# Clustered attention and a rational MoE layer on one core: new instruction sequences on every engine, and ones-matmuls over 128 rows

## The chip, the core and the metric

The kernel runs on one core of a Trainium2 chip. Five engines run their own instruction queues in order: PE (TensorE, matmuls), DVE (VectorE), ACT (ScalarE), POOL (GpSimd) and SP (SyncE, which here only issues DMAs). The metric is the device time of one execution in microseconds. Three runs of the kernel before gave 928.95, 930.76 and 934.13, median 930.76. A fourth execution was profiled; its own time is 927.86, its span in the trace 926.1.

## The reference

```python
# q, k, v: 4 batches x 8 heads x 768 tokens x 64; centroids: 8 heads x 16 x 64
q_assign = argmax(normalized(q) . normalized(centroids)); k_assign likewise
scores = (q @ k.T) / 8, set to -1e9 where q_assign != k_assign
attn   = softmax(scores);  x = attn @ v      # -> 3072 tokens x 512
h = x @ w_in                                  # 512 x 2048
P = a0 + a1*h + a2*h^2 + a3*h^3
Q = 1 + |b0|*|h| + |b1|*h^2
out = (P / (Q + 1e-6)) @ w_out                # 2048 x 512
```

## The kernel before, in words

**Tiles.** Heads are taken in four pairs per batch, tokens in six tiles of 128 per head. q and k are split into two fp16 parts with 64 further rows: the cluster of a token is written there as a one-hot row of large numbers, so that one matmul gives score and mask. `prep` does this for a pair: it loads q and k (`rk`, `rq`), squares them on ACT with a sum (`sumk`, `sumq`, tile `tk` as scratch), and finds the largest sum over the partitions. For that `over_partitions` (L960 to L968) transposes the sums on PE (`kt`, `qt`, L964), takes the maximum on DVE (`km`, `qm`, L966; tag `m1`), and spreads that one number over 128 partitions by a matmul with a row of ones (`kb`, `qb`, L968). The scale for v does the same (L785, L787, L790). Powers of two come from it (`ksc`, `qsc`), ACT and DVE write the split (`tk`, `tq`), a DMA transpose issued by SP ("turn", L1059) puts the features on the partitions (`sk`, `sq`), 48 small matmuls against the centroids give `ptl` (L1085), DVE and POOL make the one-hot `oh` of it (L1099 to L1109, L1116), and two more turns bring the second parts.

**Attention.** Batch 0 computes scores with keys on the partitions (`attend_keys`): scores for the maxima (L1301, DVE `top` L1310), the maxima written back as rows of q and turned once more, second scores `z` (L1362), exp on ACT, then `px` in fp32 (L1381, L1387). The other batches (`attend`) take 128 queries a time: scores `s` (L1181), maximum on DVE (L1197), exp on ACT with sum `su`, a split into two fp16 parts `ah` by ACT and DVE (L1234), a turn each (L1241, tile `at`), and `px` (L1254). A PSUM buffer of scores is free again when the DVE half of `ah` has read it, and two of them serve this.

**MoE.** x goes through w_in (`ph`, L1511), the rational function on ACT, DVE and POOL in pieces of 512 (`u`, `t`, `s`), and w_out (`po`, L1622). Weights are loaded and split into parts by ACT, DVE (L669 to L681) and POOL (L750, L757) in the first 200 us, beside attention of batch 0. Constants of the rational function, `g` and `gk`, are worked out one number at a time on DVE and POOL (L833, L871).

**Order.** Nothing of this runs in the order of the source. Every step is recorded with `op`: engine, an assumed duration, function, buffers read and written. `Plan.order` then brings the records into one program. A table `ORDER` holds for every engine the full list of step numbers, and each engine's steps come out in the order of its list (801 steps on PE, 1400 on DVE, 989 on ACT, 609 on POOL, 356 on SP). The assumed durations (`DMA`, `QUEUE`, `SWITCH`, the number in each `op`) then only decide which buffer of a ring a tile gets. On the chip each engine takes its list from the front and waits there for data and buffers.

Of the kernel before, what the change touches and what calls it, by code (L numbers as in the profile page):

```python
# [27 lines left out]
K = {'ghd': 0.0, 'rvp': 0, 'look': 62.89, 'mulp': 0.4, 'sub': 0, 'xn': 14, 'NR': 8, 'sgp': 1, 'scp': 1, 'vsc': 0.75, 'sup0': 0, 'stk': 2, 'lop': 0, 'mgp': 0, 'rvn': 2, 'tq2': 2, 'at': 3, 'es': 4, 'vn': 3, 'ah': 5, 'rel': 0, 'twin': 1}  # L28
# [171 lines left out]
class Plan:  # L200
# [1542 lines left out]
```

## Time and profile before

| | |
|---|---|
| runs, median (lowest to highest) | 930.76 us (928.95 to 934.13) |
| profiled execution: time, span | 927.86 us, 926.1 us |
| PE busy | 859.2 us, 93% of the span |
| DVE, ACT, POOL busy | 809.5, 763.8, 604.0 us |
| mean granted TensorE clock | 0.991 of full |
| chain that ended last | PE 28%, DVE 3%, every other engine 1% or less |

Read it by stretches: in the first 75 us PE is busy 37 us, because loads, prep and the first turns come one after the other. From 75 on it is over 90% busy, save for 50 us after 200, where batch 0's attention has ended and batch 1's begins. From 250 to 900 PE stands still for 7 us in all.

### The profile page before, as it was taken

How to read it: one execution, taken by the hardware profiler on the slowest of the kernel's cores; microseconds unless marked ns; L12 is line 12 of the kernel's file. 1: busy time of each engine (PE TensorE's matmuls, PEld its weight loads, DVE VectorE, ACT ScalarE, POOL GpSimd, SP SyncE). 2: the span in 40 equal slices, each digit the busy share in tenths (PEclk: the TensorE clock that was granted, in tenths of full speed). 3: DMA queues.
4: the chain of work that ended last, by engine and by line, in shares of the span. 5: the costliest groups of instructions: out<-in, count | busy, mean ns of one | idle time of the engine just before them, and what ended most of it. 6: DMA issues, size and time to landing. Idle time of an engine off the chain costs nothing. (4 is left out here: it accounts for less than half of the span.)

```text
span 926.1 us, 20282 instructions
## 1 busy us (share of the span) xinstructions
PE 859.2 (93%) x7705; PEld 586.4 (63%) x7705; DVE 809.5 (87%) x1618; ACT 763.8 (82%) x1182; POOL 604.0 (65%) x627
## 2 busy tenths in 40 slices
PE   1559998997999999999999999999999999999997
PEld 1346675765676666667667676666666667766664
DVE  5789899658999999999999999999999998777776
ACT  5656675878998999998999999999998898766674
POOL 1347627398888776888888788868877766322221
PEclk9979999999999999999999999999999999999999
DMA  9996774666677797886869698898758667500000
GB/s 280 295 259 186 171 172 125 184 135 148 124 131 166 138 202 145 165 168 156 157 110 201 123 168 167 173 145 169 161 107 163 123 140 107 83 24 24 1 24 23
DMA packets 357345, 132.95 MB, mean 144 GB/s; under 512 B 335104, under 2 KB 351488, under 8 KB 357248
## 3 DMA queue, kind: packets, MB, share of 16 engines
q1 hardware_dynamic: 357248, 131.67, 67.5%
q8 instruction: 60, 0.98, 0.4%
q14 instruction: 37, 0.30, 0.1%
HBM read 41.98 MB, written 6.29 MB: 52 GB/s over the span
## 5 line engine op out<-in xcount | busy, mean ns | idle before, releaser
L1622 PE MATMUL po<-wout,u 128*128 128x512 f16 x1152 | 266.1, 379 | 1.4 <-ACT ob L526 0.8
L1511 PE MATMUL ph<-x,win 128*128 128x256 f16 x2304 | 266.1, 273 | 1.2 <-DVE x L1270 0.9
L1511 PEld LDWEIGHTS <-win 128*128 128x128 f16 x2304 | 225.1, 98 | 39.7 <-issue 3.2
L1551 POOL TENSOR_TENSOR s<-s,u 128x512 f32<-128x512 f32 x96 | 131.0, 1382 | 117.9 <-ACT s L526 85.7
L1622 PEld LDWEIGHTS <-u 128*128 128x128 f16 x1152 | 111.0, 98 | 122.2 <-issue 3.4
L1234 DVE SCALAR_TENSOR_TENSOR ah<-s,su,ah 128x768 f16<-128x768 f32 x144 | 143.3, 1012 | 8.9 <-ACT ah L526 7.5
L1197 DVE TENSOR_SCALAR_CACHE_REDUCE s<-s,cc 128x768 f32<-128x768 f32 x144 | 144.6, 1018 | 7.4 <-PE s L1181 6.8
L526 ACT ACTIVATE ah<-s,su 128x768 f16<-128x768 f32 x144 | 127.1, 904 | 15.3 <-ACT s L526 7.2
L526 ACT ACTIVATE s<-s,nm 128x768 f32<-128x768 f32 x144 | 126.5, 879 | 12.8 <-DVE s L1197 9.6
L1574 POOL TENSOR_TENSOR s<-s,u 128x512 f32<-128x512 f32 x72 | 103.5, 1448 | 28.7 <-ACT u L526 28.5
L1181 PE MATMUL s<-sk,sq 128*128 128x384 f16 x576 | 113.6, 328 | 8.5 <-DVE ah L1234 3.9
L1611 POOL TENSOR_TENSOR u<-s,u 128x512 f16<-128x512 f32 x72 | 86.5, 1213 | 30.6 <-ACT u L526 16.9
L1181 PEld LDWEIGHTS <-sq 128*128 128x128 f16 x576 | 52.7, 98 | 52.3 <-DVE ah L1234 13.0
L1254 PE MATMUL px<-at,vhi 128*64 128x256 f16 x864 | 74.8, 275 | 1.2 <-DVE df L1100 0.7
L526 ACT ACTIVATE u<-ph 128x512 f32<-128x512 f32 x96 | 57.5, 601 | 19.9 <-PE ph L1511 19.4
L1532 DVE TENSOR_TENSOR t<-ph,t 128x512 f32<-128x512 f32 x96 | 65.4, 682 | 9.0 <-ACT t L526 8.7
L1254 PE MATMUL px<-at,vlo 128*64 128x256 f16 x432 | 61.3, 273 | 0.0
L1604 DVE SCALAR_TENSOR_TENSOR s<-s,t 128x1024 f32<-128x1024 f32 (+1 forms) x49 | 58.7, 1197 | 1.7 <-POOL s L1574 0.7
L1254 PEld LDWEIGHTS <-vhi 128*64 128x64 f16 x864 | 47.9, 110 | 15.7 <-issue 8.2
L526 ACT ACTIVATE u<-t 128x1024 f16<-128x1024 f32 (+1 forms) x49 | 51.2, 1045 | 6.1 <-DVE t L1594 3.0
L526 ACT ACTIVATE t<-ph,gk 128x512 f32<-128x512 f32 x72 | 56.1, 784 | 0.0
L1537 DVE SCALAR_TENSOR_TENSOR t<-t,gk,ph 128x512 f32<-128x512 f32 x72 | 53.0, 740 | 0.9
(213 smaller groups left out, 1520.7 us busy)
## 6 DMA issues: line engine op xcount, KB each, us to landing
rwi<-in_moe_w_in_dram SPq DMA_DIRECT2D x16, 512.0 KB, 5.4
rwo<-in_moe_w_out_dram SPq DMA_DIRECT2D x16, 512.0 KB, 5.4
rk<-in_k_dram SPq DMA_DIRECT2D x32, 192.0 KB, 3.3
rq<-in_q_dram SPq DMA_DIRECT2D x32, 192.0 KB, 3.0
rvm<-in_v_dram SPq DMA_DIRECT2D x16, 384.0 KB, 5.6
rv<-in_v_dram SPq DMA_DIRECT2D x16, 384.0 KB, 4.0
out_dram<-ob SPq DMA_DIRECT2D x11, 512.0 KB, 3.2
at<-ah SPq DMA_TRANSPOSE x144, 3.9
```

What stands on the lines that cost most here:

```text
L526: lambda: nc.scalar.activation(out=out(), in_=in_(), func=func, **{a: (x() if callable(x) else x) for a, x in kw.items()}),
L1181: nc.tensor.matmul(sc.ap[:, i, :SH], lhsT=st["q" + x].ap[:, j, t, :], rhs=st["k" + x].ap[:, j, ks, :].rearrange("p t c -> p (t c)"), start ...
L1197: lambda nm=nm, view=view: ts(out=view(), in0=view(), scalar1=cc.ap, scalar2=None, op0=ALU.mult, op1=ALU.min, accum_out=nm.ap),
L1234: lambda part=part, view=view, su=su: stt(out=part(1), in0=view(), scalar=su.ap, in1=part(0), op0=ALU.mult, op1=ALU.subtract),
L1254: nc.tensor.matmul(px.ap[j * D : (j + 1) * D, :], lhsT=vv.ap[:, j, kt, :], rhs=at[j].ap[:, p_, kt].rearrange("p t c -> p (t c)"), start=(i ...
L1511: nc.tensor.matmul(ph[i].ap[:, fi * TW : (fi + 1) * TW], lhsT=win[f // 4][:, wpart, c, f % 4 * P : (f % 4 + 1) * P], rhs=xs[c].ap[:, xpart ...
L1532: lambda i=i, th=th, ph=ph: tt(out=th[i].ap, in0=ph[i].ap, in1=th[i].ap, op=ALU.mult),
L1551: lambda i=i, sh=sh, uh=uh: nc.gpsimd.tensor_tensor(out=sh[i].ap, in0=sh[i].ap, in1=uh[i].ap, op=ALU.mult),
L1574: lambda i=i, sh=sh, uh=uh: nc.gpsimd.tensor_tensor(out=sh[i].ap, in0=sh[i].ap, in1=uh[i].ap, op=ALU.mult),
L1604: lambda tw=tw, sw=sw: stt(out=sw(), in0=sw(), scalar=2.0, in1=tw(), op0=ALU.subtract, op1=ALU.mult),
L1611: lambda i=i, sh=sh, gl=gl, g16=g16, e=(nc.vector if gld else nc.gpsimd): e.tensor_tensor(out=gl[i].ap, in0=sh[i].ap, in1=g16()[:, 0, i * ...
L1622: nc.tensor.matmul(po[ti].ap, lhsT=g16()[:, part, c0 : c0 + P], rhs=wout[f // 4][:, wpart, f % 4], start=(k == 0 and f == f_first), stop=( ...
```

## The change

Three things. **1.** `ORDER` is replaced by another table of the same steps: ACT has 592 of 989 steps at another place, DVE 1018 of 1400, PE 379 of 801 (none by more than 10 places), POOL 499 of 609, SP 256 of 356. The last 4 steps of PE and ACT, 12 of DVE, 8 of POOL and 9 of SP are as before. **2.** The 24 ones-matmuls that spread a maximum (20 at L968, 4 at L790) take all 128 rows of `ones`; their right side is a column of 128 numbers, zero but for the first, which DVE writes. Four such columns are set to zero once at the start. **3.** The rest of the diff is not used by this table: a PE way of turning (`by_pe`), a share of DVE (`xl`), a step `avs` that keeps its old value 3, other assumed DMA durations, and an fp16 identity that POOL copies once.

```diff
-K = {... 'twin': 1}
+K = {... 'twin': 1, 'pet': '_', 'avs': 3}
 ORDER = {
     "ACT": """
-369 370 13 383 386 7 15 39 8 17 19 34 1222 29 24 491 492 44 1224 ...
+370 369 13 1222 383 39 386 15 34 17 19 29 7 8 44 491 1224 24 25 ...
-    DMA = {"turn": (1440.0, 4100.0, 1700.0), "w": (430.0, 3900.0, 1350.0), ...
-    QUEUE = 950.0
+    DMA = {"turn": (1500.0, 4100.0, 1750.0), "w": (500.0, 4000.0, 1400.0), ...
+    QUEUE = 1300.0
+    columns = [cp.tile([P, 1], F32, name=f"column{i}") for i in range(4)]
+    def column(name):
+        return Buf(lambda i: (name, columns[i])[1], "m1", len(columns), False)
+    ident16 = cp.tile([P, P], F16, name="ident16")
+    nc.gpsimd.tensor_copy(out=ident16, in_=ident)
+    for x in columns:
+        nc.vector.memset(x, 0.0)
 @@ over_partitions (the scale of v likewise) @@
-            m1 = buf([1, 1], F32, "m1", f"{nm}m{n}", 4)
-            dve(195, lambda: nc.vector.tensor_reduce(out=m1.ap, in_=pt.ap[0:1, :], axis=AX.X, op=ALU.max), [pt], [m1], u)
+            m1 = column(f"{nm}m{n}")
+            dve(195, lambda: nc.vector.tensor_reduce(out=m1.ap[0:1], in_=pt.ap[0:1, :], axis=AX.X, op=ALU.max), [pt], [m1], u)
             pb = misc([P, 1], F32, f"{nm}b{n}")
-            op("PE", 310, lambda: nc.tensor.matmul(pb.ap, lhsT=ones[0:1, :], rhs=m1.ap, start=True, stop=True), [m1], [pb], u, mode=2)
+            op("PE", 310, lambda: nc.tensor.matmul(pb.ap, lhsT=ones, rhs=m1.ap, start=True, stop=True), [m1], [pb], u)
```

Three places show what the table moves. The first is POOL around 196 to 204 us, where it works on weights (`wwo`, `wout`), on x of batch 0 (`x0_...`) and on the constants `g11` and `g10c1`, whose results DVE waits for. Before:

```order
L1440 TENSOR_TENSOR x0_2_2_2454<-rs0_2_2_2354,x0_2_2_2454 128x256
L833 TENSOR_SCALAR g10c0_1086<-g10c0_1086 128x1
L905 TENSOR_TENSOR gk0c0_885<-gk0c0_885,aab_97 128x4
L1116 TENSOR_SCALAR tq21_0_2276<-oh1_0_2610 128x12x64
L833 TENSOR_SCALAR g10c1_2270<-g10c1_2270 128x2
L833 TENSOR_SCALAR g10c1_2270<-g10c1_2270,aab_97 128x1
L833 TENSOR_SCALAR g10c1_2270<-g10c1_2270 128x1
L757 TENSOR_TENSOR wout3_110<-wwo3_0_2095,wout3_110 128x512
L833 TENSOR_SCALAR g11_2318<-g11_2318 128x1
L1154 TENSOR_TENSOR vlo1_0_2659<-rv1_0_799,vhi1_0_2608 128x768
L1440 TENSOR_TENSOR x0_3_0_2701<-rs0_3_0_2560,x0_3_0_2701 128x256
L833 TENSOR_SCALAR g11_2318<-g11_2318,aab_97 128x1
```

After:

```order
L759 TENSOR_SCALAR wwo3_1_2180<-wwo3_1_2180,wos_124 128x512
L842 TENSOR_SCALAR g11_2406<-g11_2406 128x2
L1185 TENSOR_TENSOR vlo1_0_2626<-rv1_0_710,vhi1_0_2612 128x768
L842 TENSOR_SCALAR g11_2406<-g11_2406,aab_107 128x1
L842 TENSOR_SCALAR g11_2406<-g11_2406 128x1
L842 TENSOR_SCALAR g11_2406<-g11_2406,aab_107 128x1
L766 TENSOR_TENSOR wout3_120<-wwo3_0_2085,wout3_120 128x512
L1473 TENSOR_TENSOR x0_2_2_2697<-rs0_2_2_2361,x0_2_2_2697 128x256
L766 TENSOR_TENSOR wout3_120<-wwo3_1_2180,wout3_120 128x512
```

The last `g11` row that reads `aab` stood behind two `x0` rows and a `wout` row; now it is ahead of them.

The second is ACT around 211 to 218 us, the start of batch 1's attention: `s1_...` is the exp of a score tile, `ah1_...` the ACT half of the split behind it, `u0` and `t0` the MoE of batch 0, `tq11_2` and `vhi1_2` prep of batch 1. Before:

```order
L526 ACTIVATE x0_3_2_2840<-rs0_3_2_2727 128x256
L526 ACTIVATE s1_0_0_1_2744,su1_0_0_1_2844<-s1_0_0_1_2744,nm1_0_0_1_2768 128x2x384
L526 ACTIVATE ah1_0_0_0_2866<-s1_0_0_0_2731,su1_0_0_0_2765 128x768
L526 ACTIVATE tq11_2_2741<-rq1_2_2538,qsc1_2_2786 128x12x64
L526 ACTIVATE u0_0_0_2894<-ph0_0_0_0_2770 128x512
L526 ACTIVATE vhi1_2_2904<-rv1_2_2729,ev1_747 128x768
L526 ACTIVATE t0_0_0_2920<-ph0_0_0_0_2770,gk0c0_885 128x512
L526 ACTIVATE ah1_0_0_1_2929<-s1_0_0_1_2744,su1_0_0_1_2844 128x768
L526 ACTIVATE u0_0_0_2894<-ph0_0_0_1_2874 128x512
L526 ACTIVATE s1_0_1_0_2897,su1_0_1_0_2937<-s1_0_1_0_2897,nm1_0_1_0_2925 128x2x384
```

After:

```order
L535 ACTIVATE ah1_0_0_0_2839<-s1_0_0_0_2728,su1_0_0_0_2757 128x768
L535 ACTIVATE x0_3_2_2842<-rs0_3_2_2724 128x256
L535 ACTIVATE s1_0_0_1_2738,su1_0_0_1_2844<-s1_0_0_1_2738,nm1_0_0_1_2764 128x2x384
L535 ACTIVATE tq11_2_2735<-rq1_2_2544,qsc1_2_2762 128x12x64
L535 ACTIVATE vhi1_2_2890<-rv1_2_2726,ev1_653 128x768
L535 ACTIVATE ah1_0_0_1_2897<-s1_0_0_1_2738,su1_0_0_1_2844 128x768
L535 ACTIVATE u0_0_0_2907<-ph0_0_0_0_2825 128x512
L535 ACTIVATE t0_0_0_2924<-ph0_0_0_0_2825,gk0c0_898 128x512
L535 ACTIVATE s1_0_1_0_2899,su1_0_1_0_2929<-s1_0_1_0_2899,nm1_0_1_0_2922 128x2x384
L535 ACTIVATE u0_0_0_2907<-ph0_0_0_1_2877 128x512
```

Each `ah1` row now comes ahead of the `x0`, `u0` and `t0` rows that it followed.

The third is SP around 94 to 109 us, the second turns of batch 0's third pair (`sk20_2`, `sq20_2`) among loads. Before:

```order
L1059 DMA_TRANSPOSE sq20_1_676<-tq20_1_430 128x12x128
L1059 DMA_TRANSPOSE sq20_2_1206<-tq20_2_762 128x12x128
L1059 DMA_TRANSPOSE sk20_2_1276<-tk20_2_844 128x12x128
L1059 DMA_TRANSPOSE sk10_3_1286<-tk10_3_924 128x12x128
L540 DMA rk1_0_1294<-in_k_dram 128x384 x2
L540 DMA rv0_1_1311<-in_v_dram 128x2x384
L540 DMA rwi2_1_1314<-in_moe_w_in_dram 128x1024
L540 DMA rwi2_2_1326<-in_moe_w_in_dram 128x1024
L540 DMA rwi2_3_1351<-in_moe_w_in_dram 128x1024
```

After:

```order
L1089 DMA_TRANSPOSE sq20_1_700<-tq20_1_433 128x12x128
L549 DMA rwi2_3_1168<-in_moe_w_in_dram 128x1024
L1089 DMA_TRANSPOSE sk20_2_1203<-tk20_2_706 128x12x128
L1089 DMA_TRANSPOSE sq20_2_1220<-tq20_2_757 128x12x128
L549 DMA rk1_0_1275<-in_k_dram 128x384
L1089 DMA_TRANSPOSE sk10_3_1279<-tk10_3_931 128x12x128
L549 DMA rk1_0_1275<-in_k_dram 128x384
L549 DMA rwi2_2_1298<-in_moe_w_in_dram 128x1024
L549 DMA rwi2_1_1312<-in_moe_w_in_dram 128x1024
L549 DMA rv0_1_1321<-in_v_dram 128x2x384
```

The load `rwi2_3` stood seven places behind those two turns and stands in front of both now, and k's turn goes before q's.

## Rows read from the trace of the kernel before

**Rows 1.** Busy us by stretch: length, PE, PEld, DVE, ACT, POOL, PEclk, DMA share, GB/s
```profile
0.00:36.00 36.00, 9.45 (x85) 6.86 (x85) 22.14 (x76) 21.53 (x45) 8.60 (x25) 1.00 0.99 298
36.00:75.00 39.00, 27.45 (x191) 17.46 (x193) 33.46 (x74) 21.85 (x41) 16.93 (x21) 0.82 1.04 274
75.00:200.00 125.00, 116.80 (x1469) 84.14 (x1468) 101.53 (x217) 86.93 (x148) 72.69 (x109) 1.00 0.59 149
200.00:250.00 50.00, 40.98 (x393) 29.53 (x393) 43.53 (x103) 42.55 (x70) 42.90 (x54) 0.97 0.74 150
250.00:900.00 650.00, 643.04 (x5453) 436.55 (x5451) 591.88 (x1131) 579.12 (x865) 459.83 (x419) 1.00 0.68 131
```

**Rows 2.** PE timeline, 205:236; start us, us, engine line op, tiles, count [idle before <-releaser]
```profile
206.39 0.27 PE L964 MATMUL kt<-ident,sumk 128*1 128x128 f32 x1 [1.89 <-ACT tk L526]
...
219.15 1.26 PE L1181 MATMUL s<-sk,sq 128*128 128x384 f16 x4 [2.07 <-DVE su L1217]
220.20 4.04 PE L1511 MATMUL ph<-x,win 128*128 128x256 f16 x24
```

**Rows 3.** PE timeline around a one-row ones-matmul inside the MoE stream
```profile
259.92 1.24 PE L1622 MATMUL po<-wout,u 128*128 128x512 f16 x5
261.10 0.38 PE L968 MATMUL kb<-km,ones 1*128 1x1 f32 x2
261.40 1.04 PE L1622 MATMUL po<-wout,u 128*128 128x512 f16 x4
```

**Rows 4.** PE timeline around a 128-row ones-matmul that exists already
```profile
184.65 0.82 PE L1362 MATMUL z<-sq,sk 128*128 128x256 f16 x6
185.30 0.28 PE L708 MATMUL won<-woa,ones 128*128 128x1 f32 x2
185.44 0.81 PE L1362 MATMUL z<-sq,sk 128*128 128x256 f16 x6
```

**Rows 5.** All instructions of the line with 20 of the 24 ones-matmuls, two passes each
```profile
L968 PE MATMUL kb<-km,ones x32: 245/266/368, 9.6 to 666.6; 1*128 1x1 f32 x32
```

**Rows 6.** DVE timeline, one pass over a weight chunk at the start
```profile
17.49 0.69 DVE L674 SCALAR_TENSOR_TENSOR wwi<-rwi,wwi 128x512 int32<-128x512 int32 x1
```

**Rows 7.** PE timeline: second scores of the first pair, scores of the third pair
```profile
65.68 3.81 PE L1362 MATMUL z<-sq,sk 128*128 128x256 f16 x18
...
105.54 2.77 PE L1301 MATMUL s<-sk,sq 128*128 128x384 f16 x16
```

**Rows 8.** POOL timeline, 194:207
```profile
199.64 1.16 POOL L757 TENSOR_TENSOR wout<-wwo,wout 128x512 f16<-128x512 f32 x1
...
202.69 0.67 POOL L1440 TENSOR_TENSOR x<-rs,x 128x256 f16<-128x256 f32 x1
203.35 0.34 POOL L833 TENSOR_SCALAR g<-g,aab 128x1 f32<-128x1 f32 x1
```

**Rows 9.** DVE timeline, 203:220
```profile
203.73 0.21 DVE L871 TENSOR_SCALAR g<-g 128x1 f32<-128x1 f32 x1 [2.00 <-POOL g L833]
...
204.18 1.19 DVE L1052 COPY tk<-tk 128x768 f16<-128x768 f16 x1
...
217.02 0.69 DVE L1532 TENSOR_TENSOR t<-ph,t 128x512 f32<-128x512 f32 x1
...
218.08 1.01 DVE L1234 SCALAR_TENSOR_TENSOR ah<-s,su,ah 128x768 f16<-128x768 f32 x1
```

**Rows 10.** ACT timeline, 205:217
```profile
205.40 0.84 ACT L526 ACTIVATE tk<-rk 128x768 bf16<-128x768 f32 x1 [3.23 <-DVE tk L1052]
```

**Rows 11.** DMA issues in 199.9:201.5; the last number is the us to landing
```profile
sk<-tk SPq DMA_TRANSPOSE x1, 5.0
```

**Rows 12.** SP timeline, 92:112
```profile
99.93 4.77 SPq L1059 DMA_TRANSPOSE sk<-tk  x2
...
106.33 2.95 SPq L540 DMA_DIRECT2D rwi<-in_moe_w_in_dram  x3
```

**Rows 13.** DVE timeline, last pass over the weight chunk whose buffer that load takes
```profile
95.47 1.37 DVE L681 SCALAR_TENSOR_TENSOR wwo<-rwo,wwo 128x512 int32<-128x512 int32 x2
```

More of the change, by code (lines that the diff above doesn't have):

```diff
@@ L25 @@
 M_BIG, M_MID, M_LOW = 2.0 ** 15, 2.0 ** 7, 2.0 ** -4
-K = {'ghd': 0.0, 'rvp': 0, 'look': 62.89, 'mulp': 0.4, 'sub': 0, 'xn': 14, 'NR': 8, 'sgp': 1, 'scp': 1, 'vsc': 0.75, 'sup0': 0, 'stk': 2, 'lop': 0, 'mgp': 0, 'rvn': 2, 'tq2': 2, 'at': 3, 'es': 4, 'vn': 3, 'ah': 5, 'rel': 0, 'twin': 1}
+K = {'ghd': 0.0, 'rvp': 0, 'look': 62.89, 'mulp': 0.4, 'sub': 0, 'xn': 14, 'NR': 8, 'sgp': 1, 'scp': 1, 'vsc': 0.75, 'sup0': 0, 'stk': 2, 'lop': 0, 'mgp': 0, 'rvn': 2, 'tq2': 2, 'at': 3, 'es': 4, 'vn': 3, 'ah': 5, 'rel': 0, 'twin': 1, 'pet': '_', 'avs': 3}
 ORDER = {
     "ACT": """
[32 rows of a table removed]
[32 rows of a table added]
 """,
     "DVE": """
[45 rows of a table removed]
[45 rows of a table added]
 """,
     "PE": """
[26 rows of a table removed]
[26 rows of a table added]
 """,
     "POOL": """
[20 rows of a table removed]
[20 rows of a table added]
 """,
     "SP": """
[11 rows of a table removed]
[11 rows of a table added]
 3803 3811 3196 3925 4035 4153 4154
@@ L206 @@
     MORE = {("ACT", "POOL"): 95.0, ("DVE", "POOL"): 60.0, ("POOL", "ACT"): -30.0, ("ACT", "ACT"): 120.0, ("PE", "DVE"): 65.0, ("DVE", "ACT"): 50.0}
-    DMA = {"turn": (1440.0, 4100.0, 1700.0), "w": (430.0, 3900.0, 1350.0), "v": (450.0, 3900.0, 1100.0),
-           "qk": (430.0, 3000.0, 500.0), "few": (350.0, 2500.0, 200.0), "o2": (340.0, 3800.0, 1310.0), "o1": (340.0, 2300.0, 700.0)}
-    QUEUE = 950.0
+    DMA = {"turn": (1500.0, 4100.0, 1750.0), "w": (500.0, 4000.0, 1400.0), "v": (500.0, 4000.0, 1150.0),
+           "qk": (500.0, 3100.0, 520.0), "few": (350.0, 2500.0, 200.0), "o2": (340.0, 3800.0, 1310.0), "o1": (340.0, 2300.0, 700.0)}
+    QUEUE = 1300.0
     SWITCH = 105.0
@@ L455, in share @@
         return math.floor((i + 1) * f + 1e-6) > math.floor(i * f + 1e-6)
-    KEYMAJOR = {(0, int(hp)) for hp in kn("km", "0123")}
+    KEYMAJOR = {(0, int(hp)) for hp in kn("km", "0123") if hp != "_"}
     plan.look = kn("look", 40.0)
@@ L785, in v_scale @@
         op("PE", 110, lambda: nc.tensor.transpose(out=pt.ap[0:1, :], in_=vm1.ap, identity=ident), [vm1], [pt], vt)
-        m1 = buf([1, 1], F32, "m1", f"vmm{b}", 4)
-        dve(195, lambda: nc.vector.tensor_reduce(out=m1.ap, in_=pt.ap[0:1, :], axis=AX.X, op=ALU.max), [pt], [m1], vt)
+        m1 = column(f"vmm{b}")
+        dve(195, lambda: nc.vector.tensor_reduce(out=m1.ap[0:1], in_=pt.ap[0:1, :], axis=AX.X, op=ALU.max), [pt], [m1], vt)
         pb = misc([P, 1], F32, f"vb{b}")
         op(
-            "PE", 310, lambda: nc.tensor.matmul(pb.ap, lhsT=ones[0:1, :], rhs=m1.ap, start=True, stop=True),
-            [m1], [pb], vt, mode=2,
+            "PE", 310, lambda: nc.tensor.matmul(pb.ap, lhsT=ones, rhs=m1.ap, start=True, stop=True),
+            [m1], [pb], vt,
         )
@@ L1054, in prep, with turn, blocks, copied @@
                 )
-        def turn(x, u):
+        def turn(x, u, by_pe=False):
+            if by_pe:
+                tb_ = bank([P, 2 * NT, P], F16, "s", f"pt{x}{n}", 2)
+                def blocks(x=x, tb_=tb_):
+                    for i in range(2 * NT):
+                        nc.tensor.transpose(
+                            out=tb_.ap[:, i], in_=tm[x].ap.rearrange("p h t c -> p (h t) c")[:, i], identity=ident16
+                        )
+                def copied(x=x):
+                    return st[x].ap.rearrange("p h t c -> p (h t c)")
+                def source(tb_=tb_):
+                    return tb_.ap.rearrange("p i c -> p (i c)")
+                op("PE", 1000, blocks, [tm[x]], [tb_], u, [st[x]])
+                if x[0] == "k":
+                    act(ac(2 * NT * P, 0, True), copied, source, AF.Copy, [tb_], [st[x]], u)
+                else:
+                    dve(dc(2 * NT * P), lambda: nc.vector.tensor_copy(out=copied(), in_=source()), [tb_], [st[x]], u)
+                return
             op(
@@ L1074, in prep @@
             op("POOL", 640, fixed_rows, [], [tm["k2"], tm["q2"]], vt + kc("p2", b, 2))
+        by_pe = b == 0 and str(hp) in kn("pet", "")
         for x in ("k1", "q1"):
-            turn(x, vt + kc("p2", b, 2))
+            turn(x, vt + kc("p2", b, 2), by_pe)
         G = 4 * NT
@@ L1123, in prep @@
         for x in ("k2", "q2"):
-            turn(x, vt + kc("p4", b, 4))
+            turn(x, vt + kc("p4", b, 4), by_pe)
         if keymajor:
@@ L1263, in attend @@
         x = buf([P, 2, TW], F16, "x", f"x{n}_{tb}", kn("xn", 14))
-        for k0 in range(0, NT, 3):
-            op("PE", 1000, lambda k0=k0: av(k0, k0 + 3), [vhi, vlo, *at], [px], u, [x], mode=1)
+        step = kn("avs", 3)
+        for k0 in range(0, NT, step):
+            op("PE", 1000 * step // 3, lambda k0=k0: av(k0, k0 + step), [vhi, vlo, *at], [px], u, [x], mode=1)
         xt[b, tb, hp] = x
@@ L1346, in attend_keys @@
         )
-        turn("q2", vts[0] + 1 + kc("kdt", b))
+        turn("q2", vts[0] + 1 + kc("kdt", b), str(hp) in kn("peq", ""))
         ev = bs[b]["ev"]
@@ L1437, in attend_keys @@
             act(300, lambda x=x: x.ap[:, 0], lambda rw=rw: rw.ap, AF.Copy, [rw], [x], ux, [rs])
+            xl = share("xl", hp * NB + tb)
             op(
-                "POOL", 630,
-                lambda x=x, rw=rw: nc.gpsimd.tensor_tensor(out=x.ap[:, 1], in0=rw.ap, in1=x.ap[:, 0], op=ALU.subtract),
-                [rw], [x], ux, [rs],
+                *(("DVE", 330) if xl else ("POOL", 630)),
+                lambda x=x, rw=rw, e=(nc.vector if xl else nc.gpsimd): e.tensor_tensor(
+                    out=x.ap[:, 1], in0=rw.ap, in1=x.ap[:, 0], op=ALU.subtract
+                ),
+                [rw], [x], ux, [rs], lock=True,
             )
```

268 rows, old and new, of the table ORDER are left out of this document.

## The prediction

> **What bounds the kernel now.** I first read the busy time by stretch [rows 1], then the gaps of PE where that table shows them, then what ended each gap. PE is idle for 36.00 - 9.45 = 26.6 us in the first 36 us and for 11.6 in the next 39: there loads, prep and turns follow one another. From 75 to 200 it is idle for 8.2 of 125 us, from 200 to 250 for 9.0 of 50, from 250 to 900 for only 7.0 of 650. So two kinds of time can be won: idle time of PE, nearly all of it ahead of 250 us, and time that PE spends on something dearer than it need be. The stretch after 200 us shows what its idle time is made of [rows 2]: 1.89 us ended by ACT, 2.07 ended by DVE, and smaller ones of both kinds. DVE and ACT are busy for 43.5 and 42.6 of those 50 us [rows 1], so their order decides when PE goes on. The granted clock there has a mean of 0.97, the matmuls after the gap at 219.15 show why: 24 of 256 columns take 4.04 us, 168 ns each [rows 2], against 109 ns for such columns at the full clock, by the six z matmuls that start at 184.65 and end in 0.65 us [rows 4]. About 1.4 us go there to the lower of the two levels, 1.2 GHz in place of 2.4.
>
> **The ones-matmuls.** Each fp32 ones-matmul is two passes, and its own duration misleads: 0.38 us for the pair in one row, 0.28 for a pair that takes 128 rows already [rows 3, 4]. The starts around them tell the price. Five w_out matmuls start at 259.92. Each streams 512 columns, and four of them give 1.04 us with the last one's drain, so that one costs about 0.216; the fifth would be through at 259.92 + 5 x 0.216 = 261.00. The ones pair starts at 261.10 and the next w_out matmul at 261.40, so the one-row pair costs 261.40 - 261.00 = 0.40 us of PE's stream [rows 3]. The 128-row pair is between z matmuls: six of them from 184.65 end at 185.30, the next starts at 185.44, so it costs 0.14 [rows 4]. One changed matmul saves 0.26 at best. Where PE waits for DVE just before or behind it, less comes through. L968 runs 20 matmuls in 40 passes, 32 of them for k, the last at 666.6 us [rows 5], and 8 for q of batch 0. Of them I count 9 after 250 us, where PE waits for nothing else, at 0.15 to 0.26: 1.4 to 2.3 us; 5 between 75 and 210 us at half of it, 0.4 to 0.7; the others, ahead of 75 us and those of v, at nothing, since PE waits there for loads anyway. That is 1.8 to 3.0, **2.2 us taken**, with 1.3 to 3.5 as the range, since two places may wait for something else after all. The DVE maximum writes one number as before, and the four memsets of the columns lie in the time in which DVE waits for the first load; they cost nothing.
>
> A rule of the Trainium skill speaks against this: the page "TensorE: Matmul & The Clock Gate", section "Why this matters for your kernels", says that a lone matmul over 32 rows takes as long as one over 128, so that the gain of few rows is only in running several at once. By it, more rows would win nothing, and the sum would end at 927.9. The durations of the rows, 0.38 and 0.28, are near enough to it; the starts, 0.40 against 0.14, are not. "TensorEngine Tiling (Array Packing)", section "Tiling Modes", has a reason for the starts: a change of the tiling mode, not of the tile alone, drains the engine. No row here shows the drain itself, only the price.
>
> **The start, 0 to 75 us.** q is loaded first now and a 512 KB weight chunk stands between q and k, while DVE no longer has the centroids ahead of the first maxima. Both q and k are needed before the split can be finished, so this changes little. Before the first one-hot DVE has one more weight chunk's pass of 0.69 us [rows 6] and the cheaper step ahead of it, at most 1.4 us in all; one load fewer stands ahead of the first two turns on SP. What gates PE's steady work is the first z at 65.68 [rows 7]: it needs a row of q that DVE writes after all maxima of the first pair, and DVE's work ahead of that row is the same within 1 us. PE's gaps before it move (the maxima of the third pair come 4 us of DVE work earlier) without making z earlier. I take **0**, between -2 and +2.5.
>
> **75 to 200 us.** The orders of scores, z and px are shuffled over places a few matmuls apart. The idle 8.2 us lie in some twenty pieces, and no one of them has a cause that I see removed. I take **-0.4**, as the share of a twentieth of them, between -3 and +4: below, a third of the idle time goes; above, half as much again comes.
>
> **200 to 250 us.** The gap at 206.39 [rows 2] follows a chain that I read backwards: the transpose of sums (`kt`) waits for ACT, whose square (`tk` as scratch) started at 205.40 after 3.23 us of idling [rows 10], since it needs the `tk` buffer; DVE's copy from it ran 204.18 to 205.37, behind a `g` row on DVE that waited 2.00 us for POOL [rows 9]; POOL's `g` row ended at 203.69, behind two `x` rows, one of them 0.67, and a `wout` row of 1.16 [rows 8]. These three are behind it now, another small row of about 0.3 is ahead: 2 x 0.67 + 1.16 - 0.3 = 2.2 us earlier. But the same buffer is also read by a turn, issued at 199.9 and landed 5.0 later [rows 11], at 204.9, 0.5 before the copy ended. That is the late one next. It waits for a `sk` buffer that z matmuls hold, and those come before a small px step now. So 0.5 to 1.0 of the 1.89 is won; **0.7 taken**.
>
> The gap at 219.15 waits for a PSUM buffer, free once the DVE half of `ah` is done: 218.08 to 219.09 [rows 9]. That step stood behind `t` (217.02) and a maximum of the one-hot, 1.06 us, and needs its ACT half, which stood behind a `t` and a `u`. Both orders are turned round, so DVE can start it at 217.0, **1.1 us** earlier. The `t` and `u` that come later feed the MoE of batch 0, of which PE has 24 matmuls queued behind this score tile, so they have cover of some 24 x 0.109 = 2.6 us. The later gaps of the stretch have the same rows ahead as before; they stay. Together -1.8, and some of the low clock behind the gap, of 1.4 us, for which I count 0.2: **-2.0**, between -5 and +2.
>
> **250 to 926 us.** PE's 643 busy us [rows 1] cannot be ordered away, and of 7.0 idle us the largest pieces are below 1. **-0.5**, between -3 and +3. The last steps of all engines are unchanged: 0.
>
> **Sum.** -2.2 + 0 - 0.4 - 2.0 - 0.5 = -5.1 us. Against the profiled execution's 927.86 that is 922.8; its span is 926.1, with 1.8 around it that nothing here touches. The median of the runs is 930.76, 2.9 above the profiled execution, so I predict 930.76 - 5.1 = **925.7**.
>
> **Rivals.** *Nothing but the ones-matmuls.* A new order can win at one gap and lose at the next, since DVE and ACT are at 87% and 85% after 200 us [rows 1] and a step pulled forward delays all it passes. Then only -2.2 holds: 928.6. For it: most moves are small and on engines that wait for one another. Against it: two gaps have named causes that the order removes. *Row count without a price.* If the 0.40 us comes from two single-column fp32 passes and their loads and not from the row, 128 rows save nothing: 925.7 + 2.2 = 927.9. Against it stands the 0.14 of the other pair, which has the same passes. *The low clock goes too.* If PE's gaps after 200 us shrink enough that it keeps 2.4 GHz, and those of the first 75 us also (a mean of 0.82 from 36 to 75 us [rows 1] is 0.18 x 39 / 0.5 = 14 us at half, in which PE is busy for part of the time only), 1.2 and about 3 us more come back, and perhaps 2 of idle time: about 919.5. *A load in front of two turns (slower).* SP issues in order. The load `rwi2_3` was the last of the three that were issued from 106.33 to 109.28; the third pair's second turn for k went out at 99.93 [rows 12]. Now this load is ahead of both turns. By the old times its buffer is free at 95.47 + 1.37 = 96.8, when DVE is through with an earlier chunk [rows 13], so it should pass. If it has to wait as long as it did, both turns go out 9.4 us later; the turn at 99.93, with 5.0 to land [rows 11], is in time for the scores at 105.54 [rows 7] by 0.6, so PE loses up to 8.8 and, at half clock for a while, some 1.4 more: 925.7 + 10.2 = 935.9. It decides as soon as the load is later than 100.5.
>
> **How the numbers follow.** Forecast 0.48 (its own range 922 to 929.5), ones-matmuls alone 0.20, no price for rows 0.06, clock back as well 0.12, the load or a like wait 0.14. A measurement here tells about 0.5%, 4.65 us, from no change: faster is below 926.1, slower above 935.4. The forecast lies close to the first bound, so I give it 0.30 below and 0.18 above; with 0.12 from the clock case and 0.04 from the ones case, faster has 0.46. Same has 0.18 + 0.16 + 0.06 = 0.40, slower 0.14. The 80% range takes in the clock case and, above, the ones case and part of the slower one: 917 to 933.
>
> **What would show it.** In the changed profile the ones-matmuls inside w_in or w_out streams should leave 0.14 to 0.2 us between the neighbours' own times and no longer 0.40. The `kt` after 200 us should start at 205.4 to 205.9 on the old scale with a gap below 1.4, the fourth score tile of batch 1 about 1 us sooner, with a gap near 1. PE's idle time from 250 to 900 should stay at 5 to 8 us. SP should issue `rwi2_3` before 100 us and both turns right behind it. I am wrong if the first z moves by more than 2 us either way, if idle time of PE after 250 us grows past 10 us, or if a stretch at 1.2 GHz appears that was not there.

## The result, and the profile after

The changed kernel took 921.75 us, median of four runs (920.28 to 923.1), against 930.43 for the kernel before, run beside it (928.95 to 934.13): a ratio of 0.990, interval 0.987 to 0.993. It is faster, by 8.7 us where 5.1 were forecast; 921.75 lies inside the range of 917 to 933 and just below the 922 of the forecast's own case. Its profiled execution took 921.96 us, span 920.2. That of before was at the low end of its runs (927.86; over all comparisons here 88 runs gave 925.7 to 936.0, median 930.0), so the two traces differ by 5.9 us, less than the medians do.

Busy us by stretch of the changed kernel, in the columns of [rows 1]:

```profile
0.00:36.00 36.00, 9.69 (x87) 7.10 (x88) 23.07 (x82) 22.00 (x45) 8.51 (x26) 1.00 0.97 287
36.00:75.00 39.00, 25.52 (x177) 16.25 (x178) 30.61 (x70) 21.00 (x39) 13.92 (x20) 0.74 1.01 266
75.00:200.00 125.00, 119.37 (x1500) 86.76 (x1500) 103.48 (x226) 90.08 (x154) 83.02 (x113) 1.00 0.64 161
200.00:250.00 50.00, 43.28 (x424) 31.28 (x421) 46.04 (x105) 44.86 (x71) 44.05 (x54) 0.97 0.73 142
250.00:900.00 650.00, 642.41 (x5441) 437.54 (x5440) 594.46 (x1130) 580.23 (x867) 451.44 (x416) 1.00 0.68 130
```

Against [rows 1], PE is busy 1.9 us less from 36 to 75, 2.6 us more in the next 125, 2.3 us more from 200 to 250, and 0.6 less behind. So what lies between 75 and 250 us won. That the start lost is not shown: in a second trace of the changed kernel (the run "once more" below) PE is busy for 36.5 of the first 75 us, where it was 35.2 in the first trace and 36.9 in the kernel before. The second trace:

```profile
0.00:36.00 36.00, 10.40 (x89) 7.48 (x90) 23.97 (x84) 22.48 (x45) 8.64 (x27) 1.00 0.98 293
36.00:75.00 39.00, 26.08 (x186) 16.70 (x184) 31.27 (x72) 21.76 (x40) 14.72 (x21) 0.78 1.04 267
```

PE's timeline of the changed kernel (first trace) after 200 us answers to [rows 2]:

```profile
203.02 0.27 PE L973 MATMUL kt<-ident,sumk 128*1 128x128 f32 x1 [0.74 <-ACT tk L535]
...
214.48 0.81 PE L1212 MATMUL s<-sk,sq 128*128 128x384 f16 x4 [0.73 <-DVE ah L1265]
215.86 2.79 PE L1546 MATMUL ph<-x,win 128*128 128x256 f16 x24 [0.57 <-DVE t L1572]
...
221.38 0.82 PE L1212 MATMUL s<-sk,sq 128*128 128x384 f16 x4 [2.08 <-DVE ah L1265]
222.04 4.45 PE L1546 MATMUL ph<-x,win 128*128 128x256 f16 x24
...
256.49 0.28 PE L977 MATMUL kb<-column,ones 128*128 128x1 f32 x2
```

The ones-matmul in the last line starts at 261.10 in [rows 3], so 4.6 of the 5.9 us between the traces are won by there. Both named gaps shrank, from 1.89 to 0.74 and from 2.07 to 0.73. The gap of 2.08 is not a new one: it stands ahead of the sixth score tile of batch 1, and that tile waited for as long in the kernel before:

```profile
226.95 0.82 PE L1181 MATMUL s<-sk,sq 128*128 128x384 f16 x4 [2.05 <-DVE ah L1234]
```

What moved is the stretch at the lower clock. It lay behind the fourth score tile, where 24 `ph` matmuls took 4.04 us [rows 2], and lies behind the sixth now, where 24 take 4.45. The mean granted clock of the 50 us is 0.97 in both traces.

The chain ahead of the first gap in the changed kernel answers to [rows 8 to 10]. POOL's timeline:

```profile
197.95 0.34 POOL L842 TENSOR_SCALAR g<-g,aab 128x1 f32<-128x1 f32 x1
```

DVE's timeline there:

```profile
198.33 0.21 DVE L880 TENSOR_SCALAR g<-g 128x1 f32<-128x1 f32 x1 [0.30 <-POOL g L842]
...
198.65 0.98 DVE L1061 COPY tk<-tk 128x768 f16<-128x768 f16 x1
```

And ACT's:

```profile
202.03 0.84 ACT L535 ACTIVATE tk<-rk 128x768 bf16<-128x768 f32 x1 [2.91 <-DMA sk<-tk]
```

DVE's `g` row waits 0.30 for POOL in place of 2.00. What ACT waits for is now the turn from the same buffer, the one that the prediction called late next.

### The profile page after: what moved, and what is told of

It is laid out like the page before. It is cut to its first block, busy times and chain, and to the rows that moved or that the text cites. A ratio compares the mean times of both kernels' runs of the same rounds, so it can differ in the third digit from the quotient of the medians.

```text
span 920.2 us, 20304 instructions
## 1 busy us (share of the span) xinstructions
PE 855.8 (93%) x7705; PEld 586.9 (64%) x7705; DVE 809.0 (88%) x1622; ACT 765.5 (83%) x1182; POOL 603.9 (66%) x628
## 5 line engine op out<-in xcount | busy, mean ns | idle before, releaser
L1228 DVE TENSOR_SCALAR_CACHE_REDUCE s<-s,cc 128x768 f32<-128x768 f32 x144 | 144.9, 1018 | 6.8 <-PE s L1212 6.3
L1646 POOL TENSOR_TENSOR u<-s,u 128x512 f16<-128x512 f32 x72 | 84.6, 1185 | 35.1 <-DVE s L1639 20.1
L1285 PEld LDWEIGHTS <-vhi 128*64 128x64 f16 x864 | 45.7, 110 | 15.3 <-issue 7.3
```

The lines of the kernel that those rows point to most:

```text
L1228: lambda nm=nm, view=view: ts(out=view(), in0=view(), scalar1=cc.ap, scalar2=None, op0=ALU.mult, op1=ALU.min, accum_out=nm.ap),
L1285: nc.tensor.matmul(px.ap[j * D : (j + 1) * D, :], lhsT=vv.ap[:, j, kt, :], rhs=at[j].ap[:, p_, kt].rearrange("p t c -> p (t c)"), start=(i ...
L1646: lambda i=i, sh=sh, gl=gl, g16=g16, e=(nc.vector if gld else nc.gpsimd): e.tensor_tensor(out=gl[i].ap, in0=sh[i].ap, in1=g16()[:, 0, i * ...
```

## The experiments

All times below are medians beside the kernel before on the same chip, in four comparisons in which it took 930.1, 930.0, 929.6 and 929.9 us. A ratio is worked out from all runs and need not be the quotient of the two medians; behind it stands its 95% interval. "Old" and "new" are the sequences of before and of the change. My theory was that the ones-matmuls bring their 2.2 us, that the new sequences bring the rest in stretches that each pay by itself, and that the new start costs 1.5 us. The rivals: the ones-matmuls bring nothing; the parts pay only together.

**The ones-matmuls alone**, on the old sequences.

```diff
-  m1 = buf([1, 1], ...);  matmul(lhsT=ones[0:1, :], rhs=m1.ap)
+  m1 = column(...)        # 128x1, zero but for row 0
+  matmul(lhsT=ones, rhs=m1.ap)
```

> The kernel before with the 24 ones-matmuls over 128 rows and its old sequences. Theory (the drain around a one-row matmul is what costs): 2.2 us less than the kernel before (1.3 to 3.5), ratio about 0.9976; L968 pairs in the MoE stream take 0.15 to 0.2 us of PE in place of 0.40. Rival (the price is that of two single-column fp32 passes, whatever the rows): no difference, ratio 0.9995 to 1.0005, pairs still at 0.40.

Measured: 931.39 us, ratio 1.0011 (0.9991 to 1.003). The predicted gain of 2.2 us would be 0.9976 and lies outside. The price in the stream did fall, as [rows 3, 4] had it; PE's timeline of this kernel:

```profile
258.97 1.46 PE L1629 MATMUL po<-wout,u 128*128 128x512 f16 x6
260.26 0.28 PE L975 MATMUL kb<-column,ones 128*128 128x1 f32 x2
260.40 1.46 PE L1629 MATMUL po<-wout,u 128*128 128x512 f16 x6
```

260.40 - 260.26 = 0.14 us. Measured over all pairs after 75 us by such starts, with the waits right beside them, their prices fell from 6.8 to 4.2 us. In the two profiles PE's idle pieces of over 0.15 us between 75 and 250 us grew meanwhile, from 16.1 to 17.7; the wait for `tk` at 109 us, for one, from 1.17 to 1.67:

```profile
109.36 0.27 PE L971 MATMUL kt<-ident,sumk 128*1 128x128 f32 x1 [1.67 <-ACT tk L533]
```

Behind 250 us little of it came through either. From the pair at 261.10 to the last one the kernel before takes 405.3 us, and this kernel takes 405.1 from 260.26 to its last one, though the pairs on the way cost some 1.4 us less. PE's waits between them grew from 5.6 to 6.2 us, which is half of what is missing. The last pair in PE's timeline before:

```profile
666.44 0.38 PE L968 MATMUL kb<-km,ones 1*128 1x1 f32 x2
```

And in this kernel's:

```profile
665.35 0.28 PE L975 MATMUL kb<-column,ones 128*128 128x1 f32 x2
```

**The new sequences alone**, with one-row ones-matmuls.

```diff
-  lhsT=ones, rhs=m1.ap        # m1 = column(...)
+  lhsT=ones[0:1, :], rhs=m1.ap  # m1 = buf([1, 1], ...)
```

> The changed kernel with one-row ones-matmuls as before. Theory (the sequences bring the larger part, the ones-matmuls 2.2 us): about 6.5 us less than the kernel before, ratio 0.993. Rival (the ones-matmuls bring most, or the two gains depend on one another): less than 4 us below the kernel before.

Measured: 920.4 us, 0.9892 (0.9865 to 0.9919). The whole gain is in the sequences. The changed kernel itself, run **once more**:

```diff
 (the changed kernel, not edited)
```

> The changed kernel once more, for more runs of it and a second profile: 921.75 us from four runs, the same with one-row ones-matmuls 920.4 from six. Theory A (128 rows cost nothing and bring nothing): 920 to 921. Theory B (128 rows cost 1 to 1.5 us by more time at the half clock, as the means of four and six runs say): 921.5 to 922.

921.0 us, 0.9904 (0.9883 to 0.9924): not to be told from 920.4 in another comparison. Neither a gain nor a cost of the 128 rows is shown.

**Only the start new; all but the start new.** Both with 128-row ones-matmuls; 931.39 is their base.

```diff
-  ORDER = new
+  ORDER = new for steps that begin before 74 us, then old   # start new
+  ORDER = old for steps that begin before 74 us, then new   # start old
```

> 128-row ones-matmuls; new sequences for all steps that the changed kernel starts before 74 us, old ones for the rest. Theory (the new start is 1.5 us later at the first z, since the last row of q stands behind a weight chunk's first step on DVE that waits for a load): 0 to 1.5 us less than the kernel before, the ones-matmuls' 2.2 less what the start loses. Rival (the gain of 75 to 200 us is prepared by the start, which loads the pieces in another order): 4 us less or better.

> 128-row ones-matmuls; old sequences for all steps that the kernel before starts before 74 us, new ones for the rest. Theory (the start costs 1.5 us, the gain is later): 1 to 2 us below the changed kernel, 9.5 to 11 below the kernel before. Rival (start and middle belong together): 2 us or more above the changed kernel.

Measured: start new 932.08 (1.0025, 1.0008 to 1.0043), start old 924.25 (0.9937, 0.9916 to 0.9958). The first fits: by itself the new start is worth nothing or costs a little. The second contradicts my theory: without the start that costs, the kernel should have beaten the changed one, and it is 2.5 us slower than the changed kernel's 921.75 (the intervals of the two ratios, 0.9916 to 0.9958 and 0.987 to 0.993, overlap a little). So the rival held, and I had to cut the rest as well, on the code of before. I had called the other assumed DMA durations of the change unused, but they choose buffers, and the code of before has the old ones. Worked out from the two programs, under the old durations the new sequences have another tile ahead in the same buffer in 2 of 1758 cases. So this hardly sets the cut kernels apart; no run tests it by itself.

**Only the middle new, only the end new; start and middle, start and end.**

```diff
-  ORDER = old
+  ORDER = old up to 74 us, new up to 200, then old   # middle
+  ORDER = old up to 200 us, then new                 # end
+  ORDER = new up to 200 us, then old                 # start and middle
+  ORDER = new up to 74 us, old up to 200, then new   # start and end
```

> The kernel before (one-row ones-matmuls, 930.1 us) with only the operations between 74 and 200 us put in the new sequences; those ahead and behind keep the old. Theory A (each stretch pays by itself): the PE time lost between 75 and 200 us, some 3.7 us less in the changed kernel by the two profiles, comes through: 926 to 927.5 us. Theory B (a stretch pays only with the one that follows it): 929 to 931, with the gain given back as waits between 200 and 260 us.

> The kernel before with the new sequences only for operations behind 200 us. Theory A (each stretch pays by itself): 2.0 us from the two gaps before the sumk matmuls around 203 and 215 us, and 1.5 to 2 from the expert stretch behind 250 us: 926 to 927. Theory B (the late gain hangs on the order ahead of it): 929 to 931. With the middle kernel: if both gains add up to the 6 us that the old start with the new rest brought (924.25 against 930.1), stretches are independent; if the sum is under 3 us, they are not.

> The kernel before (one-row ones-matmuls, 930.0 us) with the new sequences for all operations up to 200 us and the old behind. The parts so far, against their own base: start alone +0.7 to +0.9, middle alone -2.9 (medians; -0.24% by the ratio), late alone -1.3 (-0.25%), all of them -9.7. Theory A (the parts add up, and the missing 5 us is the spread of single runs): 927 to 929. Theory B (start and middle belong together: the landings that the new start brings are those for which the middle is ordered): 922 to 925, so most of the gain is here.

> The kernel before with the new start (up to 74 us), the old middle and the new sequences from 200 us on. Theory A (the parts add up): 929 to 930. Theory B (start and middle belong together, late pays by itself): 928.5 to 930 too, so this kernel tells a third case apart: theory C (start and late order belong together, the middle is carried along): 922 to 925.

| new sequences in | median us | ratio (interval) |
|---|---|---|
| start (128 rows) | 932.08 | 1.0025 (1.0008 to 1.0043) |
| middle | 927.15 | 0.9976 (0.9956 to 0.9996) |
| end | 928.77 | 0.9975 (0.9953 to 0.9997) |
| start and end | 928.09 | 0.9985 (0.9969 to 1.0002) |
| start and middle | 924.2 | 0.9941 (0.9918 to 0.9964) |
| middle and end (128 rows) | 924.25 | 0.9937 (0.9916 to 0.9958) |
| all | 920.4 | 0.9892 (0.9865 to 0.9919) |

The single parts add up to -0.24% (+0.25 - 0.24 - 0.25, or -0.35% if the +0.11% of the 128-row base is taken off the start); all together bring -1.08%. Each pair that holds the middle brings some 0.6%, and the pair without it 0.15%. Taken in pairs, middle and end add up within their intervals (-0.49% as single parts, -0.63% together), and so do start and end (0 and -0.15%). Start and middle do not: 0 as single parts and -0.59% together, and with the end's -0.25% that is -0.84%, within the noise of the whole. So neither "each stretch pays by itself" nor "only together" is the whole truth. Middle and end pay something alone, and what no part has alone needs the new start and the new middle together, as theory B of the third of these expectations had it.

The traces show which waits go with which part. Each trace is one execution, and not always one near the median: that of the middle alone took 922.04 us, the lowest of its twelve runs, that of start and middle 927.34, near the highest of its seven. So their waits tell what a part takes away or brings, and can't be added up to the medians. With the old middle PE waits for `tk` at 109 us and for a px step at 174 (1.17 and 1.29 us). PE's timeline of the kernel before, at two places not shown yet:

```profile
109.49 0.27 PE L964 MATMUL kt<-ident,sumk 128*1 128x128 f32 x1 [1.17 <-ACT tk L526]
...
174.28 0.71 PE L1424 MATMUL px<-rs,pick 128*128 128x128 f32 x4 [1.29 <-DVE rs L1416]
```

Middle alone new, PE:

```profile
108.91 0.27 PE L967 MATMUL kt<-ident,sumk 128*1 128x128 f32 x1
...
202.32 0.27 PE L967 MATMUL kt<-ident,sumk 128*1 128x128 f32 x1 [0.80 <-ACT tk L529]
...
214.62 0.81 PE L1184 MATMUL s<-sk,sq 128*128 128x384 f16 x4 [2.06 <-DVE su L1220]
```

End alone new, PE:

```profile
110.86 0.27 PE L967 MATMUL kt<-ident,sumk 128*1 128x128 f32 x1 [1.54 <-ACT tk L529]
...
207.39 0.27 PE L967 MATMUL kt<-ident,sumk 128*1 128x128 f32 x1 [1.52 <-DVE rs L1435]
...
220.61 0.81 PE L1184 MATMUL s<-sk,sq 128*128 128x384 f16 x4 [0.74 <-DVE ah L1237]
...
228.10 0.82 PE L1184 MATMUL s<-sk,sq 128*128 128x384 f16 x4 [2.66 <-DVE ah L1237]
```

The middle takes away the wait at 109 and brings the one at 206 [rows 2] down to 0.80; its cause stands ahead of 200 us. The end takes most of the wait for the score tile, 2.07 to 0.74. All fourteen traces agree: the waits at 109 and at the px step are there in the five with the old middle (1.17 to 1.67 and 0.90 to 1.89 us) and gone in the nine with the new one, and the wait at 206 is 1.52 to 2.15 with the old middle, 0.62 to 0.91 with the new. And seams, the places where an old and a new stretch meet, make waits longer: the end behind the old middle has 2.66 us at 228 where the whole change has 2.08, and start and end together wait 1.89 for the px step and 2.15 for `tk`:

```profile
176.49 1.10 PE L1427 MATMUL px<-rs,pick 128*128 128x128 f32 x4 [1.89 <-DVE rs L1419]
...
210.36 0.27 PE L967 MATMUL kt<-ident,sumk 128*1 128x128 f32 x1 [2.15 <-ACT tk L529]
```

One seam of start and middle is a landing. With the old start ahead of the new middle, the z matmuls at 171 us wait for a turn of q; middle and end new, PE:

```profile
172.30 1.36 PE L1397 MATMUL z<-sq,sk 128*128 128x256 f16 x11 [1.02 <-DMA sq<-tq]
```

This turn took 6.1 us to land there, the last number of its DMA issue:

```profile
sq<-tq SPq DMA_TRANSPOSE x1, 6.1
```

With all sequences new and one-row ones-matmuls, the same turn:

```profile
sq<-tq SPq DMA_TRANSPOSE x1, 4.2
```

With middle alone it took 5.8 and PE waited 0.74; with start and middle 4.5, and PE did not wait. The same turn was issued at 165.8 to 167.1 in all four. In all seven traces with a new start and the new middle it took 4.2 to 4.7 us and PE did not wait for it; with the old middle it took 5.9 to 6.4, whatever the start. Why it lands later behind the old start is not shown. This is the one wait found that goes with start and middle together, and it is worth 1 us at most. Such waits explain a microsecond here and there, not all of the some 7 us by which the whole exceeds the sum of its parts.

**A start put in order by hand**, on the new sequences with one-row ones-matmuls. In the changed kernel PE waits 8.12 us before it goes on at 62.63, and the last row of q for z stands on DVE behind two weight passes that wait for ACT (0.94 and 1.53 us). Steps 423, 425 are the last maxima, 430 that row, 431 its turn, 432 to 438 the z groups, 433 to 439 their exp.

```diff
 DVE -616 104 519 2217 621 423 622 76 425 77 426 78 1235 427 107 428 429 81 430 82 ...
 DVE +616 519 2217 425 423 426 427 428 429 430 104 621 622 76 77 78 1235 107 81 82 ...
 SP  -522 110 431        +431 522 110
 PE  -2220 3206 84 3208 86 432 434 436 ...   +432 434 436 2220 3206 438 84 3208 86 ...
 ACT -80 3204 2221 ... 433 435    +80 433 3204 435 2221 437 ...
```

> The changed kernel with one-row ones-matmuls (920.4 us here) and a start reordered further: DVE makes the last row of q for the second score matmul of batch 0 (61.58 us in the changed kernel) ahead of four weight rounding steps that wait for ACT and for loads, its turn is issued ahead of another turn, and PE runs three z matmul groups before the v and norm work. Theory A (PE's 8.1 us wait before 62.6 us is lost time, and work brought forward stays won): first z at about 60 us in place of 67.2, the wait about 5.5 us, the whole 917 to 918.5 us. Theory B (what follows, the loads of w_in landing at 68.8 us and the turns of the next heads, sets the time from 75 us on): the first z moves as much, but the operations at 100 us stand where they stood to within 1 us, the whole 920 to 921.5. Theory C (start and later order are fitted to each other, as when the old start was put before the new rest): above 922.

Measured: 929.23 us, 0.9984 (0.9968 to 1.0), 8.8 us more than without it: theory C. DVE's timeline of this kernel:

```profile
54.62 0.20 DVE L1379 TENSOR_SCALAR tq<-rest 128x12 f16<-128x12 f32 x1
...
65.38 0.16 DVE L795 TENSOR_REDUCE vm<-vm 128x1 f32<-128x4 f32 x1 [4.00 <-ACT rvm L538]
```

SP's, the turn of that row:

```profile
55.90 2.48 SPq L1092 DMA_TRANSPOSE sq<-tq  x1
```

PE's, the z groups and a weight's norm:

```profile
62.37 3.78 PE L1397 MATMUL z<-sq,sk 128*128 128x256 f16 x17 [6.27 <-DMA sq<-tq]
...
77.66 0.41 PE L707 MATMUL wig<-wwi 128*128 128x128 bf16 x4 [2.74 <-DVE wwi L693]
```

ACT's, the exp that was moved ahead:

```profile
63.63 0.90 ACT L538 ACTIVATE at<-z,cc 128x768 f32<-128x768 f32 x1 [3.61 <-PE z L1397]
```

DVE made the row at 54.62 in place of 59.67, 5 us sooner. Its turn landed only 2.1 us sooner (62.32 for 64.42), since it was issued 4.0 sooner, behind a load that went out at 55.41 only, and took 6.4 us in place of 4.5, with three loads, 1.3 MB together, just ahead of it. The page "DMA: Bandwidth & Descriptors" of the Trainium skill, section "Queues, rings and completion order", says that each DMA engine takes one issuer's descriptors in the order of its ring; the later landing behind those loads agrees with it. Then exp, put early on ACT, waited 3.61 us for z, a step for v behind it came late, DVE waited 4.00 for that, and PE 2.74 for weights at 77.66. By the profiles PE stands 6 us behind at 85 us and 8 at 250. The start is held by landings (a DMA share of 1.0 in the windows) and by what ACT and DVE do between them; the 8.12 us could not be won in this way.

**A hand at the gap that is left.** The 2.08 us at 221.38 and the half clock behind it look like 3 us to be won. On the new sequences with one-row ones-matmuls, twice. Steps 1333, 1341, 1349 are score tiles, 1327 and 1339 free their buffers, 887 and 888 are `ph` matmuls, 885 and 886 the DVE steps that free the px bank, 872 a product of 2.39 us, 1329 and 1330 px.

```diff
 DVE -1324 1434 1325 862 1334 1327 863 1336 885 1342 1337 872 1339 1344 1345 886
 DVE +1324 1325 862 863 1327 1334 885 1434 1336 1337 1342 1339 872 1344 1345 886   # first
 DVE +1324 1325 862 863 1327 1334 885 886 1434 1336 1337 1342 1339 872 1344 1345   # second
 PE  -1333 1341 887 888 1349 1329 1330
 PE  +1333 887 1341 888 1349 1329 1330   # first
 PE  +1333 887 1341 888 1329 1330 1349   # second
 ACT -861 883 1326 884 1335 868 869 1338   +861 1326 883 884 868 1335 1338 869
```

> The changed kernel with one-row ones-matmuls (920.4 us) and, at 217 to 225 us only, 8 DVE, 5 ACT and 2 PE operations moved past one another: the expert matmul 887 goes ahead of score matmul 1341, the probabilities that free its bank go ahead of a new maximum, and the 2.39 us DVE product ahead of the probabilities goes behind them. Theory A (that wait of PE, 2.08 us, and the half clock behind it, 3.4 us in which 1.7 us are lost, are lost time): the wait falls to about 1 us, the clock stays up, 917.5 to 919. Theory B (DVE and ACT bound this stretch and any order gives the same): the wait comes back within 10 us, 920 to 921.

> The kernel of the gap fix with its second fault taken away. There, the probabilities' px matmuls waited 2.40 us for DVE's step 886, which frees their bank and stood behind the 2.39 us product, and score matmul 1349 waited 1.93 us. Now 886 stands right behind its twin 885, and the px matmuls go ahead of 1349. Theory A (the waits between 217 and 232 us come from the places of single steps): they fall from 5.3 us there, and 3.76 us with the refined sequences alone, to about 2.5, the clock stays up, and the whole is 918 to 919.5. Theory B (DVE and ACT have no room in this stretch, what one step gains the next loses): they stay at 3.5 or more, and the whole is 920 to 924.

Measured: 924.18 us (0.993, 0.9912 to 0.9949) and 924.03 (0.9932, 0.9907 to 0.9958), both above 920.4 (0.9892). PE's timeline of the first:

```profile
217.59 1.49 PE L1549 MATMUL ph<-x,win 128*128 128x256 f16 x12 [0.99 <-DVE t L1575]
...
222.96 0.82 PE L1215 MATMUL s<-sk,sq 128*128 128x384 f16 x4 [1.93 <-DVE ah L1268]
226.18 0.64 PE L1288 MATMUL px<-at,vhi 128*64 128x256 f16 x4 [2.40 <-DVE t L1575]
```

PE's of the second:

```profile
218.50 1.48 PE L1549 MATMUL ph<-x,win 128*128 128x256 f16 x12 [1.00 <-DVE t L1575]
...
223.17 0.38 PE L1288 MATMUL px<-at,vhi 128*64 128x256 f16 x3 [1.00 <-DMA at<-ah]
...
230.30 1.18 PE L1215 MATMUL s<-sk,sq 128*128 128x384 f16 x4 [4.25 <-DVE ah L1268]
```

DVE's of the second, the steps ahead of that last wait:

```profile
224.39 2.40 DVE L1632 SCALAR_TENSOR_TENSOR t<-t,gk0c,u 128x1024 f32<-128x1024 f32 x1
...
228.09 1.23 DVE L1642 SCALAR_TENSOR_TENSOR s<-s,t 128x1024 f32<-128x1024 f32 x1
229.24 1.01 DVE L1268 SCALAR_TENSOR_TENSOR ah<-s,su,ah 128x768 f16<-128x768 f32 x1
```

The aimed wait halved each time and came back within 12 us, larger: 3.76 us of waits between 217 and 232 with the new sequences became 5.3 and 6.25. Nor did the clock stay up. By stretch, in the columns of [rows 1], the first has a mean granted clock of 0.57 behind its waits:

```profile
223.00:231.00 8.00, 5.60 (x44) 4.42 (x45) 6.47 (x10) 4.87 (x8) 7.00 (x7) 0.57 1.01 150
```

The product of 2.40 us has to be done somewhere, and DVE of the second has no gap over 0.3 us from 215 to 230. Theory B held, and its penalty was larger than I gave it. None of the kernels tried beats the new sequences as they stand.

## Why the prediction was right, and where not

- **The sum, -5.1 for -8.7.** The sign and the two named gaps were right; the size came from elsewhere than I put it. That the time lay in the range is in part luck: 2.2 us that did not come were outweighed by gains that I had priced at nothing or nearly so. Of the sequences alone I expected -2.9, and they bring some 9.7.
- **The ones-matmuls, -2.2: wrong, 0.** The price per matmul was read rightly from the starts (0.40 to 0.14 us, shown); that it would come through was the failed step: the interval of the ones-matmuls alone ends at -0.09%, and the kernel that leaves them out has the full gain. I had counted the nine after 250 us at 1.4 to 2.3 us because PE waits for nothing else there. Their prices did fall by 1.6 us in the trace, but PE does wait between them (5.6 us in all, 6.2 with 128 rows); where the rest went is not settled. The page "TensorE: Matmul & The Clock Gate" of the Trainium skill, section "Why this matters for your kernels", says that a lone matmul over 32 rows takes as long as one over 128. The time of this kernel came out as that rule would have it, the place in PE's stream did not: between fp16 neighbours the pair in 128 rows cost 0.14 us and in one row 0.40.
- **The start, 0 (-2 to +2.5): right alone, wrong in company.** Alone it is +0.25%. The first z came 1.48 us later, at 67.16, in the first trace of the changed kernel, but at 65.90 in the second and at 65.27 with one-row ones-matmuls, where it was 65.68 before; so a later first z is not shown. Ahead of the new middle and end the new start is worth 3.2 us (924.25 to 921.0, 0.9937 to 0.9904, both with 128 rows). I treated the stretches as independent terms.
- **75 to 200 us, -0.4: the step most in error.** I said that no piece of the 8.2 us idle had a cause that I saw removed. The middle alone brings 0.24%, with the start in front of it 0.59%. Its idle time fell by 2.6 us, from 8.2 to 5.6. Two of its pieces, 1.17 us for ACT's `tk` and 1.29 for a px step, were large enough to be followed as I followed the two after 200 us, and both are gone with the new middle.
- **200 to 250 us, -2.0.** At the 206 us gap 0.7 of 1.89 was forecast and 1.15 came, by the chain that was read: POOL, `g`, copy, `tk`, with the turn as the next late one. Its cause belongs to the part ahead of 200 us. The score tile's gap lost 1.34 for 1.1. "The later gaps stay" was wrong in its details (2.05 and 1.23 became 2.08 and 0.64, and one of 0.57 came), right in sum. The 0.2 for the clock did not come.
- **250 to 926 us, -0.5.** PE is idle for 7.6 of 650 us where it was 7.0, so nothing was won in its idle time there. A stretch at the lower clock that was not there before came at 372 (in the second trace at 370), which I had named as a sign of being wrong; by its 4 us at a mean clock of 0.57 it costs under 2 us, and it did not decide.

```profile
372.00:376.00 4.00, 3.88 (x14) 1.45 (x15) 3.96 (x9) 3.92 (x6) 2.57 (x3) 0.57 0.39 115
```

- **The slower rival did not happen.** SP of the changed kernel: the load goes out at 96.13, near the 96.8 that [rows 13] gave, and both turns behind it before or at 100.2.

```profile
96.13 0.76 SPq L549 DMA_DIRECT2D rwi<-in_moe_w_in_dram  x1
98.45 1.67 SPq L1089 DMA_TRANSPOSE sk<-tk  x1
100.21 1.47 SPq L1089 DMA_TRANSPOSE sq<-tq  x1
```

What stays open: why start and middle bring so much more together. Beside the waits shown at the seams, single runs of mixed sequences spread more (a standard deviation of 2.0 to 2.8 us for middle, end and their pairs, 2.1 for before) than those of the whole change (1.1 over ten runs). That would fit sequences chosen over several sets of landings, but the start alone had 1.4, the start by hand 1.1, and the second try at the gap, with nearly all steps in the new order, 2.3; no experiment here settles it.

## What to carry to other kernels

Follow every wait of the bounding engine over 1 us back to its cause, also in a stretch with many small ones, and look for that cause ahead of the stretch where the wait stands. Orders of neighbouring stretches need not add up: to say what a part is worth, try it with its neighbours in both forms. Where the engines behind PE are busy without a gap, moving a few steps to close a wait can merely move the wait, as it did twice here, and an instruction made cheaper in the stream is worth nothing until a run of the whole shows it. A single trace tells which wait has gone; what it is worth is told by many runs.

## What the runs showed of the hardware

The time of single runs goes with the granted clock. In the four comparisons a run of the kernel before that spent 1 us more at half the clock (worked out from its mean clock) was 0.23 to 0.36 us longer, with correlations of 0.57 to 0.88; in the first of them this time went from 13 to 35 us over 29 runs. Whether the clock makes these runs longer, or whatever makes them longer also lowers the clock, is not shown. And the landing of one and the same turn differed by 1.9 us (4.2 to 6.1) between kernels whose SP issued the same loads and turns in the 25 us before it.
